# Segmented attention beside a 2-D Fourier filter: head stacks read in rows of 8 KB, and an output projection in 14 products

## The chip, the core and the metric

The kernel runs on one core of a Trainium2 chip. A core has a matrix engine (TensorE, PE in the profile, with its weight loads as PEld), a vector engine (VectorE, DVE), a scalar engine (ScalarE, ACT), GpSimd (POOL) and SyncE (SP), which does nothing here but start DMA transfers. Sixteen DMA engines move data between the device's memory (DRAM) and the on-chip memory SBUF. SBUF has 128 partitions (rows); matrix products land in PSUM, which the vector and scalar engines read. The metric is the device time of one execution in microseconds (us), lower is better.

## The reference, cut to what matters

Two independent parts stand side by side in the output. Part B multiplies a 2048 x 576 input by a filter in the space of a two-dimensional Fourier transform; the kernel computes it with matrix products against tables, and the change does not touch it. Part A is attention in four segments of 512 positions with a compressive memory, 32 heads of width 18:

```python
q,k,v = x@wq, x@wk, x@wv            # each reshaped to 32 heads x 4 segments x 512 x 18
for s in range(4):
    logits = einsum("bhqd,bhkd->bhqk", qs, ks)*scale + mask
    p = softmax(logits);  a_dot = einsum("bhqk,bhkd->bhqd", p, vs)
    pq = phi(qs)                                     # phi(t) = t+1 if t>0 else exp(t)
    a_mem = einsum(pq, M) / (einsum(pq, z) + 1e-6)   # memory of the earlier segments
    o = g*a_mem + (1-g)*a_dot
    M = M + einsum(phi(ks), vs);  z = z + sum(phi(ks))
out_A = concat(o) @ wo                               # 2048 x 576
out_B = irfft2(rfft2(xB) * (w_r + 1j*w_i))
out = concat([out_A, out_B], axis=-1)
```

The weights of the queries and keys are drawn large, so logits are large and the products must be close to float32.

## The kernel before

**Stages.** The Fourier part's forward half fills the first 73 us. Then come the projections (`projections`, line 533): for each of the four segments g, nine column tiles of 128 of the joined query and key weights (`qk_unit`, line 461), and four row tiles of the values. They end at about 282 us. Then the inverse Fourier half runs, with the first steps of the attention beside it from 294 us (the first product of line 637), and from 355 us (the first of line 682) to the end attention is all that runs (`attention`, line 913).

**Split numbers.** To get the precision of float32 out of bf16 products, each query and key value is cut in three bf16 parts, high, middle and low, which `qk_unit` writes to a tile `sp3` of 128 rows x 3 x 512 and stores in DRAM as `qkD` (line 486). The product of a query and a key is made of six of the nine part products. So that one matrix product does them all, the six pieces of 18 rows each are stacked on 108 partitions: the query stack `Qs` has parts (h,h,h,m,m,l), the key stack `Ks` parts (h,m,l,h,m,h) (`stack_dmas`, line 612). A stack holds 8 heads of a segment; there are 16 query stacks and 16 key stacks, n = 0 to 15. Each is filled by six transfers of 18 partitions, with eight pieces of 1 KB per partition (one per head). Three query and four key buffers rotate. In the trace the first buffers of both carry the name `x`.

**Attention's loop.** A step t of `attention` treats one head of one segment: `s2` makes the logits, transposed, from `Ks` and `Qs` and takes the exponential; `pv` multiplies with the values; `s1`, ten steps ahead, makes the logits a first time for the row maxima. The maxima of four heads go through GpSimd, a transpose on TensorE and a copy (`mpath`, line 655) into a tile `mts`, from which a small transfer on ScalarE's own DMA queue (line 672, 8 KB) puts them on partitions 108 and 109 of the query stack, where `s2` needs them about three steps later. Every eight steps a new n begins; its stack loads are appended to a list `q` (lines 936 to 938: queries for n+2, keys for n+3, then the values), and each step takes up to two off the list. They are issued on SP's queue, in program order, beside the stores of results (`uD`, `rD`), the loads for the memory path (`pq`, `ux`, `rr`, `rd`) and the output stores.

**Memory path and output.** `mixed` (line 794) combines the segment before (`combine`) and computes the memory term of this one (`mem1`) over five row tiles t of heads, 126 rows for t < 4 and 72 for t = 4. `combine` leaves the result split in two parts that TensorE takes at float32r, `oh` (high) and `ol` (rest). `oproj` (line 837) multiplies with the output weights, split likewise into `woh` and `wol` (`late_setup`, line 595): three products (oh woh, oh wol, ol woh) for each of the five tiles, 15 into one PSUM tile of 128 x 288, eight such units per segment, for segments 0 to 2. Half a unit is issued per background turn (`run_bg`). The last segment has its own code (`last_tile`, `last_proj`).

The order of all instructions is that in which the code issues them (`manual_schedule`), for each engine apart; engines meet at semaphores.

## Time and profile before

| what | us |
|---|---|
| median of 3 runs (717.62 to 721.08) | 720.45 |
| the profiled execution | 718.92 |
| its span, first to last instruction | 717.2 |
| TensorE busy (share of the span) | 684.1 (95%) |
| VectorE busy | 552.3 (77%) |
| ScalarE busy | 450.1 (63%) |
| GpSimd busy | 211.1 (29%) |

The span is 1.7 us shorter than the profiled execution, and that execution is 1.5 us below the median. A row of a view of groups or of the timeline names the line, the engine, the operation, and the tiles as out<-in; "x5" counts instructions put together. A bracket at its end is the time that the engine stood idle before it, and what ended that. A list of waits gives who waited for whom: total us, times, longest. Matrix products are pipelined: the next starts before the one before has ended, so the spacing of starts, not the duration, is the cost of one.

### The profile page before, as it was taken

To read this page: it belongs to the slowest core of one execution; us is meant where nothing else is said; L and a number is where in the kernel's file an instruction comes from. 1 tells how busy PE (TensorE), PEld (TensorE's weight loads), DVE (VectorE), ACT (ScalarE), POOL (GpSimd) and SP (SyncE) were. 2 spreads that over 40 slices of the span, in tenths; PEclk is the share of its full clock that TensorE was granted. 3 is DMA by queue.
4 is the path that set the end of the run, shared out by engine and by line. 5 is a ranking of instruction groups with operands and counts; after the bars stand their busy time and mean duration, and the time that the engine had idled before them with its cause. 6 is when DMAs were issued, how large, how long until landed. Compare 5 with 4: busy or idle time off the path is not lost. (4 is left out here: it accounts for less than half of the span.)

```text
span 717.2 us, 14460 instructions
## 1 busy us (share of the span) xinstructions
PE 684.1 (95%) x5007; PEld 505.7 (71%) x5007; DVE 552.3 (77%) x1270; ACT 450.1 (63%) x985; POOL 211.1 (29%) x403
## 2 busy tenths in 40 slices
PE   4999999999999999999999899899999999999997
PEld 4988869879779879999854444444466445664497
DVE  5999979899699789788588787878466876568633
ACT  3665796585586575444487677767466776567521
POOL 5432000100200111665154333435123662235300
PEclk9999999999999999999999999999999999999999
DMA  8995435645363568899547665776446775441152
GB/s 305 293 280 164 148 118 185 192 169 182 110 220 147 178 198 281 208 231 228 165 111 174 171 172 136 185 173 170 114 126 158 195 169 126 126 137 42 28 153 83
DMA packets 83304, 121.02 MB, mean 169 GB/s; under 512 B 11472, under 2 KB 50750, under 8 KB 83096
## 3 DMA queue, kind: packets, MB, share of 16 engines
q1 hardware_dynamic: 76580, 104.11, 50.3%
q0 software_dynamic: 5632, 15.76, 8.0%
q8 instruction: 39, 0.64, 0.4%
q10 hardware_dynamic: 1020, 0.25, 0.2%
q14 instruction: 33, 0.27, 0.1%
HBM read 81.78 MB, written 38.24 MB: 167 GB/s over the span
## 5 line engine op out<-in xcount | busy, mean ns | idle before, releaser
L641 DVE CUSTOM_DVE_ANT_0 junk<-s,x 128x512 bf16<-128x512 f32 (+1 forms) x256 | 141.4, 552 | 67.2 <-PE s L637 62.0
L696 POOL TENSOR_SCALAR_AFFINE_SELECT P<-P 128x512 f32<-128x512 f32 (+2 forms) x132 | 78.8, 623 | 67.3 <-ACT P L683 51.8
L647 DVE TENSOR_REDUCE mx<-s 128x4 f32<-128x512 f32 x128 | 87.7, 686 | 2.9 <-PE s L646 0.7
L683 ACT ACTIVATE P<-s 128x512 f32<-128x512 f32 x128 | 76.4, 597 | 16.5 <-PE s L682 5.4
L711 PE MATMUL pv<-P,vs 128*32 128x512 f32 (+3 forms) x1024 | 82.8, 441 | 0.0
L692 ACT ACTIVATE P<-s 128x256 f32<-128x256 f32 x128 | 49.4, 386 | 49.7 <-PE s L691 49.6
L688 ACT ACTIVATE P<-s 128x512 f32<-128x512 f32 x128 | 76.1, 594 | 2.0 <-PE s L687 1.8
L637 PE MATMUL s<-Ks,Qs 108*128 108x384 bf16 (+3 forms) x256 | 69.1, 301 | 1.2 <-DVE mx L647 0.9
L711 PEld LDWEIGHTS pv<-P,vs 128*32 128x32 f32 x1024 | 27.2, 109 | 45.3 <-issue 42.5
L459 PE MATMUL pj<-x,wqkh 128*128 128x512 f32 x162 | 56.5, 409 | 0.0
L205 DVE TENSOR_TENSOR Z<-t,t 128x290 f32<-128x290 f32 (+1 forms) x96 | 48.4, 554 | 0.1
L637 PEld LDWEIGHTS <-Qs 108*128 108x128 bf16 x320 | 31.5, 98 | 22.6 <-issue 11.3
L506 POOL MEMSET vt<- 128x32 f32 x16 | 2.4, 166 | 149.1 <-PE pm L516 127.7
L205 DVE TENSOR_TENSOR t<-Z 128x580 f32<-128x580 f32 x64 | 46.0, 755 | 0.0
L142 PE MATMUL f<-ftab,eh 128*128 128x290 f32 (+1 forms) x160 | 32.5, 322 | 12.1 <-DMA ftab<-ftab 9.5
L646 PE MATMUL s<-tri,idb 128*128 128x128 bf16 x256 | 43.2, 220 | 0.0
L295 PE MATMUL i<-civ,Y 128*128 128x256 f32 (+1 forms) x288 | 39.0, 288 | 0.2 <-POOL Y L280 0.2
L295 PEld LDWEIGHTS i<-civ,Y 128*128 128x128 f32 (+1 forms) x288 | 36.4, 181 | 1.0 <-POOL Y L280 0.4
L306 PE MATMUL i<-itab,T 128*128 128x290 f32 (+1 forms) x224 | 36.3, 305 | 0.1
L637 PE MATMUL s<-Ks,x 108*128 108x384 bf16 (+3 forms) x128 | 35.3, 306 | 1.1 <-DVE mx L647 0.6
L142 PEld LDWEIGHTS f<-ftab,eh 128*128 128x128 f32 (+1 forms) x160 | 26.2, 207 | 14.1 <-issue 8.5
L459 PE MATMUL pj<-x,wqkl 128*128 128x512 f32 x90 | 35.5, 395 | 0.0
(203 smaller groups left out, 1820.8 us busy)
## 6 DMA issues: line engine op xcount, KB each, us to landing
qkD<-sp SPq DMA_DIRECT2D x36, 384.0 KB
Ks<-qkD SPq DMA_DIRECT2D x72, 144.0 KB
x<-qkD SPq DMA_DIRECT2D x60, 144.0 KB
Qs<-qkD SPq DMA_DIRECT2D x60, 144.0 KB
xin<-xb SPq DMA_DIRECT2D x16, 384.0 KB
cfw<-cfw POOLq DMA_DIRECT2D x16, 384.0 KB, 4.4
civ<-civ POOLq DMA_DIRECT2D x16, 384.0 KB, 7.6
vs<-vD SPq DMA_DIRECT2D x16, 330.0 KB
```

Of the source, the lines that this page charges most:

```text
L142: nc.tensor.matmul(p[:,r,:FP],x,t,start=n==0,stop=n==6)
L205: v.tensor_tensor(o,a,b,op=op)
L295: nc.tensor.matmul(p[:m,k],Y[i][:,q,c*128:c*128+m],cc[:,hl,o:o+256],start=n==0,stop=n==5)
L459: s.nc.tensor.matmul(out,a,b,start=i==0,stop=i==len(L)-1)
L637: nc.tensor.matmul(out,Q[:108,h,128*i:128*i+128],K[:108,h,:128*(i+1)],start=True,stop=True)
L641: nc.vector.tensor_tensor_reduce(out=junk[:,:w],in0=src,in1=s.mask[:,512-w:],scale=1.0,scalar=-3.0e38, op0=OP.add,op1=OP.max,accum_out=s.m ...
L647: nc.vector.tensor_reduce(out=s.mx[k][:,hh],in_=pa.rearrange("p (b c) -> p b c",c=128),axis=mybir.AxisListType.X,op=OP.max)
L683: nc.scalar.activation(P[0][:,hh],p0,AF.Exp,scale=SC)
L688: nc.scalar.activation(P[1][:,hh],p1,AF.Exp,scale=SC)
L692: nc.scalar.activation(P[2][:,hh],p2,AF.Exp,scale=SC)
L696: nc.gpsimd.affine_select(out=x[:,r],in_=x[:,r],pattern=[[0,r.stop-r.start],[1,128]],compare_op=OP.is_ge,fill=0.0,base=0,channel_multiplie ...
L711: nc.tensor.matmul(s.pvt[32*hh:32*hh+32,128*j:],vt[:,j,19*h:19*h+32],mv[0][:,hh,mv[1]],start=j==0,stop=j>1,skip_group_check=True)
```

## The change

**Query and key columns are permuted on the host** so that a tile of 128 columns holds sixteen of the 18 dimensions of 8 heads, ordered dimension by head; the two dimensions left over of all 32 heads, of the queries and of the keys, make up tile 4. In DRAM, `qkD` is laid out by group of heads and by part, and the left-over rows go to a second array `reD`, once for each place that they have in a stack (six stores instead of one for tile 4). **A stack** is then filled by four transfers: 48, 32 and 16 partitions from `qkD` and 12 from `reD`, each partition one piece of 8 KB that holds all eight heads. The parts of a key are stored in reversed order, so that the same six part products arise. Stack 0 is loaded in four turns of the hook instead of six. The store of phi(q), the transposed phi(k) and their layout follow the permutation (`pqD`, `pk`).

**The output projection** has its tile 4 rearranged: the 56 rows that were empty beneath the 72 rows of `oh` take the first 56 rows of `ol`, and a second tile holds a copy of `oh`'s 72 rows and the last 16 of `ol`; the weights are doubled to match. So three products of tile 4 become two, and a unit has 14. Rows move across partitions by three transfers from SBUF to SBUF per segment. `combine`, `mem1` and the loads for them treat the tiles in the order 4, 0, 1, 2, 3 (`ORD`).

```diff
@@ -339,6 +339,7 @@
 BF=mybir.dt.bfloat16
+ORD=(4,0,1,2,3)
 H=32; DH=18; SC=float(DH)**-0.5
@@ -356,9 +357,9 @@
 def host_wo(w):
-    o=np.zeros((126,5,D),np.float32)
-    o[:,:4]=w[:504].reshape(4,126,D).transpose(1,0,2)
-    o[:72,4]=w[504:]
+    o=np.zeros((128,6,D),np.float32)
+    o[:126,:4]=w[:504].reshape(4,126,D).transpose(1,0,2)
+    o[:72,4]=w[504:]; o[72:,4]=w[504:560]; o[72:88,5]=w[560:]
     return o
@@ -389,7 +390,8 @@
         d=lambda n,sh,dt: dp.tile(sh,dt,name=n)
-        s.qkD=[d(f"qkD{i}",[1152,3,512],BF) for i in range(4)]
+        s.qkD=[d(f"qkD{i}",[8,3,128,512],BF) for i in range(4)]
+        s.reD=[d(f"reD{i}",[24,32,512],BF) for i in range(4)]
         s.pqD=[None]+[d(f"pqD{i}",[576,512],F32) for i in range(1,4)]
@@ -468,31 +470,42 @@
         if (g==0 and mt<4) or (g==3 and mt>4): r1=r0
-        nc.scalar.copy(sp3[:,0],ps)
+        j=[2,1,0] if mt>4 else [0,1,2]
+        nc.scalar.copy(sp3[:,j[0]],ps)
         if r1>r0:
...
         if r1>r0: nc.vector.scalar_tensor_tensor(e[r0:r1],ps[r0:r1],0.0,e[r0:r1],op0=OP.max,op1=OP.add)
-        nc.vector.tensor_tensor(ps,ps,sp3[:,0],op=OP.subtract)
+        nc.vector.tensor_tensor(ps,ps,sp3[:,j[0]],op=OP.subtract)
         qr=min(r1,128 if mt<4 else (64 if mt==4 else 0))
-        if qr>r0: nc.sync.dma_start(s.pqD[g][128*mt:128*mt+qr],e[:qr])
-        yield
-        nc.scalar.copy(sp3[:,1],ps)
-        yield
-        nc.tensor.matmul(ps,s.nid,sp3[:,1],start=False,stop=True,skip_group_check=True)
-        nc.scalar.copy(sp3[:,2],ps)
-        nc.sync.dma_start(s.qkD[g][128*mt:128*mt+128],sp3)
+        if qr>r0:
+            a=s.pqD[g][0]
+            J=[(18*8*mt*512,[[512,16],[18*512,8]],e[:qr])] if mt<4 else [((16+j)*512,[[18*512,32]],e[32*j:32*j+32]) for j in range(2)]
+            for o,ap,x in J: nc.sync.dma_start(bass.AP(tensor=a.tensor,offset=a.offset+o,ap=ap+[[1,512]]),x)
+        yield
+        nc.scalar.copy(sp3[:,j[1]],ps)
+        yield
+        nc.tensor.matmul(ps,s.nid,sp3[:,j[1]],start=False,stop=True,skip_group_check=True)
+        nc.scalar.copy(sp3[:,j[2]],ps)
+        if mt!=4: nc.sync.dma_start(s.qkD[g][mt-(mt>4)].rearrange("i p c -> p i c"),sp3)
+        else:
+            for r,i,c,n in ((0,0,1,3),(0,1,1,2),(0,2,1,1),(64,0,3,3),(64,0,2,2),(64,0,1,1)):
+                m={3:0,2:3,1:5}[n]; a=s.reD[g][r*12//64+2*m]
+                x=sp3[r:r+64,i:i+c] if c==n else sp3[r:r+64,i:i+1].to_broadcast([64,n,512])
+                nc.sync.dma_start(bass.AP(tensor=a.tensor,offset=a.offset,ap=[[512,64],[64*512,n],[1,512]]),x)
         if r1<=r0: return
...
         if k0>=r1: return
-        n=r1-k0; c0=128*mt+k0-576
+        n=r1-k0
         pt=pp.tile([128,4,128],F32,name="ptr",tag="pt")
...
         yield
-        nc.scalar.copy(s.pk[:,:,c0:c0+n],pt[:,:,:n])
+        pk=s.pk.rearrange("p a (h d) -> p a h d",d=18)
+        if mt==4: nc.scalar.copy(pk[:,:,:,16:],pt[:,:,:n].rearrange("p a (d h) -> p a h d",d=2))
+        else: nc.scalar.copy(pk[:,:,8*mt-40:8*mt-32,:16],pt.rearrange("p a (d h) -> p a h d",h=8))
     def v_unit(s,g,tb,tp,pp):
@@ -596,31 +609,34 @@
         s.sel=cp.tile([96,5,126],BF,name="sel",bufs=1); nc.gpsimd.dma_start(s.sel,io["sel"].rearrange("p (t m) -> p t m",t=5))
-        s.woh=cp.tile([126,5,576],F32R,name="woh",bufs=1); s.wol=cp.tile([126,5,576],F32R,name="wol",bufs=1)
-        for t in range(6):
-            if t>1: yield
-            if t<5:
-                x=cp.tile([128,576],F32,name="ob")[:126]; q.append(x)
+        s.woh=cp.tile([128,5,576],F32R,name="woh",bufs=1); s.wol=cp.tile([128,5,576],F32R,name="wol",bufs=1)
+        for t in (0,1,2,3,5,4,6):
+            if t: yield
+            if t<6:
+                x=cp.tile([128,576],F32,name="ob"); q.append((t,x))
                 nc.sync.dma_start(x,io["wo"][:,576*t:576*t+576])
-            for _ in range(2): yield
-            if t>0:
-                x=q.pop(0)
-                nc.scalar.copy(s.woh[:,t-1],x)
-                nc.gpsimd.tensor_tensor(s.wol[:,t-1],x,s.woh[:,t-1].bitcast(F32),op=OP.subtract)
+            yield
+            if t!=5: yield
+            if len(q)>(t<6):
+                u,x=q.pop(0)
+                if u==5: nc.scalar.copy(s.wol[64:96,4],x[64:96]); continue
+                r=128 if u<4 else 72
+                nc.scalar.copy(s.woh[:,u],x)
+                nc.gpsimd.tensor_tensor(s.wol[:r,u],x[:r],s.woh[:r,u].bitcast(F32),op=OP.subtract)
         yield
...
         L=[]
-        T,base,order=((s.Qs[n%3],0,(0,0,0,1,1,2)),(s.Ks[n%4],576,(0,1,2,0,1,0)))[qk]
-        for pc,o in enumerate(order):
-            a=s.qkD[g][base+8*G*18:base+8*G*18+18,o]
-            ap=bass.AP(tensor=a.tensor,offset=a.offset,ap=[[1536,18],[1536*18,8],[1,512]])
-            def go(T=T,pc=pc,ap=ap):
-                nc.sync.dma_start(T[18*pc:18*pc+18],ap)
-                if pc==5: s.loaded.add((n,qk))
-            L.append(go)
+        T=(s.Qs[n%3],s.Ks[n%4])[qk]
+        u=G+4*qk
+        for p0,i0,i1 in ((0,0,3),(48,qk,2+qk),(80,2*qk,1+2*qk)):
+            L.append(lambda p0=p0,i0=i0,i1=i1: nc.sync.dma_start(T[p0:p0+16*(i1-i0)].rearrange("p a c -> p (a c)"),s.qkD[g][u,i0:i1].rearrange("i (d h) c -> (i d) (h c)",h=8)))
+        def go():
+            nc.sync.dma_start(T[96:108],s.reD[g][12*qk:12*qk+12,8*G:8*G+8])
+            s.loaded.add((n,qk))
+        L.append(go)
         return L
@@ -798,7 +814,7 @@
             if i>=d:
-                for _ in s.mem1(g,i-d): yield
+                for _ in s.mem1(g,ORD[i-d]): yield
     def ux_load(s,g,t):
@@ -812,16 +828,21 @@
             r=126 if u<4 else 72
-            s.oh[u]=tp.tile([126,512],F32R,name="oh",bufs=5); s.ol[u]=tp.tile([126,512],F32R,name="ol",bufs=5)
+            s.oh[u]=tp.tile([128,512],F32R,name="oh",bufs=5); s.ol[u]=tp.tile([128,512],F32R,name="ol",bufs=5)
             (nc.vector.tensor_copy if s.now>=119 else nc.scalar.copy)(s.oh[u][:r],s.am[u][:r])
...
             r=126 if u<4 else 72
-            eng().tensor_tensor(s.ol[u][:r],s.am[u][:r],s.oh[u][:r].bitcast(F32),op=OP.subtract)
+            A,B=s.oh[u],s.ol[u]
+            l=B if u<4 else tp.tile([128,512],F32R,name="ol4",bufs=1)
+            eng().tensor_tensor(l[:r],s.am[u][:r],A[:r].bitcast(F32),op=OP.subtract)
+            if u==4:
+                s.later(1,lambda: nc.sync.dma_start(B[:72].bitcast(F32),A[:72].bitcast(F32)))
+                s.later(2,lambda: (nc.sync.dma_start(A[72:128].bitcast(F32),l[:56].bitcast(F32)),nc.sync.dma_start(B[72:88].bitcast(F32),l[56:72].bitcast(F32))))
         late=g==2
         for t in range(7+late):
-            if t>1 and not late: high(t-2); low(t-2)
+            if t>1 and not late: high(ORD[t-2]); low(ORD[t-2])
             if t<5:
-                r=126 if t<4 else 72; x=xs[t]
+                i=t; t=ORD[t]; r=126 if t<4 else 72; x=xs[t]
                 pb=s.post("pb")
@@ -830,9 +851,10 @@
                     eng().tensor_tensor(s.am[t][:r],x[:r],s.am[t][:r],op=OP.add)
-                if t<2: s.later(1,lambda t=t: s.ux_load(g,t+3))
-            if late and 1<t<7: high(t-2)
-            if late and t>2: low(t-3)
+                t=i
+                if t<2: s.later(1,lambda t=t: s.ux_load(g,ORD[t+3]))
+            if late and 1<t<7: high(ORD[t-2])
+            if late and t>2: low(ORD[t-3])
             yield
@@ -843,11 +865,10 @@
                 w=slice(288*hf,288*hf+288)
-                L=[(a,b,t) for a,b in ((oh,s.woh),(oh,s.wol),(ol,s.woh)) for t in range(5)]
-                for i,(a,b,t) in enumerate(L):
-                    r=126 if t<4 else 72
-                    nc.tensor.matmul(ps,a[t][:r,c],b[:r,t,w],start=i==0,stop=i==14)
-                    if i==7: yield
+                L=[(a,b,t,126) for a,b in ((oh,s.woh),(oh,s.wol),(ol,s.woh)) for t in range(4)]+[(oh,s.woh,4,128),(ol,s.wol,4,88)]
+                for i,(a,b,t,r) in enumerate(L):
+                    nc.tensor.matmul(ps,a[t][:r,c],b[:r,t,w],start=i==0,stop=i==13)
+                    if i==6: yield
                 nc.scalar.copy(ob[:,w],ps)
@@ -909,7 +930,7 @@
 
-        for n,t,b in (("oh",F32R,5),("ol",F32R,5),("am",F32,5),("pq",F32,5),("ux",F32,3)): s.tp.tile([128 if b==3 else 126,512],t,name=n,bufs=b)
+        for n,t,b in (("oh",F32R,5),("ol",F32R,5),("am",F32,5),("pq",F32,5),("ux",F32,3),("ol4",F32R,1)): s.tp.tile([128 if n in ("oh","ol","ux","ol4") else 126,512],t,name=n,bufs=b)
     def attention(s,tp,ps):
@@ -937,14 +958,14 @@
             st=t%32
-            if 16<=t<21: s.pq_load(1,t-16)
+            if 16<=t<21: s.pq_load(1,ORD[t-16])
             if t==34: bg.append(s.den(1,lane))
...
                         next(r); yield
-                    for u in range(3): s.ux_load(g-1,u)
+                    for u in range(3): s.ux_load(g-1,ORD[u])
                     yield from r
@@ -1045,8 +1066,11 @@
     f=lambda a: np.asarray(a,np.float32)
-    return dict(xa=host_xa(f(x)),wqk=host_wt(np.concatenate([f(wq),f(wk)],1)).reshape(128,-1),wv=host_wt(f(wv)).reshape(128,-1),
-        wo=host_wo(f(wo)).reshape(126,-1),beta=np.repeat(f(beta),4).reshape(128,1),**atables())
+    h,d=np.arange(32),np.arange(16)
+    m=[((8*G+h[None,:8])*18+d[:,None]).ravel() for G in range(4)]; r=(h*18+16+d[:2,None]).ravel()
+    wqk=np.concatenate([f(wq)[:,np.concatenate(m+[r])],f(wk)[:,np.concatenate([r]+m)]],1)
+    return dict(xa=host_xa(f(x)),wqk=host_wt(wqk).reshape(128,-1),wv=host_wt(f(wv)).reshape(128,-1),
+        wo=host_wo(f(wo)).reshape(128,-1),beta=np.repeat(f(beta),4).reshape(128,1),**atables())
 def emit(nc,tc,io):
@@ -1080,7 +1104,7 @@
                     if g==3 and i==3: A.masks()
-                    if g==3 and 0<i<7:
+                    if g==3 and 0<i<5:
                         for _ in range(2): q0.pop(0)()
```

In these excerpts of the order, a row is a line, an operation, the tiles as out<-in and the shape; equal neighbours are counted ("x6").

SP's queue at the start of the block n = 3 (its loads fill a query buffer and a key buffer, here `Qs_3293` and `Ks_3295`, after the change `Qs_3316` and `Ks_3318`), before:

```order
L621 DMA Qs_3293<-qkD_71 18x8x512 x6
L621 DMA Ks_3295<-qkD_71 18x8x512 x3
L722 DMA rD_3305<-U 4x2x512
L621 DMA Ks_3295<-qkD_71 18x8x512
L727 DMA uD_3301<-U 18x2x512
L621 DMA Ks_3295<-qkD_71 18x8x512
L727 DMA uD_3301<-U 18x2x512
L621 DMA Ks_3295<-qkD_71 18x8x512
L727 DMA uD_3301<-U 18x2x512
L628 DMA vs<-vD_78 128x4x165
L727 DMA uD_3301<-U 18x2x512
```

The same place on SP's queue after:

```order
L635 DMA Qs_3316<-qkD_71 48x4096
L635 DMA Qs_3316<-qkD_71 32x4096
L635 DMA Qs_3316<-qkD_71 16x4096
L637 DMA Qs_3316<-reD_75 12x4096
L635 DMA Ks_3318<-qkD_71 48x4096
L635 DMA Ks_3318<-qkD_71 32x4096
L635 DMA Ks_3318<-qkD_71 16x4096
L637 DMA Ks_3318<-reD_75 12x4096
L644 DMA vs<-vD_82 128x4x165
L738 DMA rD_3328<-U 4x2x512
L743 DMA uD_3324<-U 18x2x512 x4
```

Both stacks now stand ahead of the store of the sums (`rD`), which waits for the result copy `U`; before, three of the twelve loads stood behind it.

TensorE's queue in the output projection of segment 2, two units, before:

```order
L849 MATMUL po<-woh,oh 128x288 x5
L849 MATMUL po<-wol,oh 128x288 x5
L849 MATMUL po<-woh,ol 128x288 x5
L849 MATMUL po<-woh,oh 128x288 x5
L849 MATMUL po<-wol,oh 128x288 x5
L849 MATMUL po<-woh,ol 128x288 x5
```

The same two units after:

```order
L870 MATMUL po<-woh,oh 128x288 x4
L870 MATMUL po<-wol,oh 128x288 x4
L870 MATMUL po<-woh,ol 128x288 x4
L870 MATMUL po<-woh,oh 128x288
L870 MATMUL po<-wol,ol 128x288
L870 MATMUL po<-woh,oh 128x288 x4
L870 MATMUL po<-wol,oh 128x288 x4
L870 MATMUL po<-woh,ol 128x288 x4
L870 MATMUL po<-woh,oh 128x288
L870 MATMUL po<-wol,ol 128x288
```

Tile 4 has moved from the fifth place of each group of five to two products at the end of the unit.

The three moves of rows for segment 0 on SP's queue, after (before, these rows are not there, and the loads of `pq` and the stack follow the stores of `uD` directly):

```order
L743 DMA uD_3325<-U 18x2x512 x2
L839 DMA ol<-oh 72x512
L743 DMA uD_3325<-U 18x2x512
L840 DMA oh<-ol_6394 56x512
L840 DMA ol<-ol_6394 16x512
L772 DMA pq<-pqD_79 72x512
L635 DMA x_2754<-qkD_72 48x4096
```

The moves stand ahead of a `pq` load and of the next block's stack loads.

## The prediction

> **What bounds the kernel now.** I read the page's engine row, then busy time by stage, then TensorE's waits in the attention.
>
> ```profile
> PE 684.1 (95%) x5007; PEld 505.7 (71%) x5007; DVE 552.3 (77%) x1270; ACT 450.1 (63%) x985; POOL 211.1 (29%) x403
> 20.00:360.00 340.00, 334.54 (x2137) 295.86 (x2137) 292.81 (x562) 213.26 (x427) 69.67 (x144) 1.00 0.64 194
> 365.00:505.00 140.00, 132.11 (x1159) 65.89 (x1157) 113.19 (x340) 104.85 (x253) 58.26 (x108) 1.00 0.65 162
> 510.00:556.00 46.00, 46.00 (x396) 31.27 (x394) 26.95 (x79) 27.53 (x67) 13.32 (x28) 0.98 0.50 131
> 597.00:645.00 48.00, 47.96 (x406) 32.05 (x408) 29.25 (x85) 29.86 (x72) 13.77 (x30) 1.00 0.47 128
> 677.00:717.00 40.00, 35.47 (x261) 33.44 (x261) 14.62 (x23) 8.75 (x21) 2.92 (x6) 0.99 0.34 109
> ```
>
> The last five rows are stages: length, busy time of PE, PEld, DVE, ACT, POOL, then the granted clock, the mean busy share of the 16 DMA engines and GB/s. TensorE is the bound, busy 95% of the span at full clock. It never stops in the two stretches that hold the output projections of segments 0 and 1 (46.00 of 46.00, 47.96 of 48.00). In 365 to 505 us it stands idle for 7.9 us. What it waits for from 365 to 690 us:
>
> ```profile
> PE s L682 <- DMA Qs<-mts: 3.2, 3, 1.4
> PE pd L765 <- DMA pq<-pqD: 1.4, 1, 1.4
> PE pb L826 <- DMA rr<-rrD: 1.2, 1, 1.2
> PE s L637 <- DMA Qs<-qkD: 0.4, 1, 0.4
> PE s L682 <- DMA x<-mts: 0.2, 1, 0.2
> ```
>
> These five rows, 6.4 us, are all waits for transfers. So two things can move the time: fewer products where TensorE is full, and transfers that land sooner or later than the step that needs them.
>
> **One product less per unit.** Three segments have eight units each, so 24 products go. Their price is the spacing of starts:
>
> ```profile
> 681.04 0.83 PE L849 MATMUL po<-woh,oh 126*128 126x288 f32 x5
> 681.70 0.82 PE L849 MATMUL po<-wol,oh 126*128 126x288 f32 x5
> 682.37 0.83 PE L849 MATMUL po<-woh,ol 126*128 126x288 f32 x5
> 683.03 0.30 PE L849 MATMUL po<-woh,oh 126*128 126x288 f32 x1
> ...
> 689.34 0.69 DVE L859 TENSOR_TENSOR ux<-ux,pb 126x512 f32<-126x512 f32 x1 [8.48 <-DMA ux<-uD]
> 691.82 0.40 PE L849 MATMUL po<-woh,oh 126*128 126x288 f32 x1 [0.16 <-ACT ob L851]
> ```
>
> Fifteen products take 683.03 - 681.04 = 1.99 us, 0.133 each. In the two full stretches 16 products are worth 2.1 us. Segment 2's eight units lie in the tail. There VectorE waits until 689.34 for `ux`, ScalarE's copies that free the accumulators stand behind the work that follows, and TensorE meets that at 691.82. So the six units ahead of 691.82 end sooner for nothing: the wait grows by their 0.8 us. The two units behind it give 0.27. The term is -2.4; its ends are -2.1 (tail nothing) and -3.2 (all 24).
>
> **The three moves of rows, and the new tile order.** The first low part is made on GpSimd at 471.7 us and the first product that could read it starts at 512.2:
>
> ```profile
> L819 POOL TENSOR_TENSOR ol<-am,oh x10: 1260/1268/1282, 471.7 to 593.1; 126x512 fp32r<-126x512 f32 x8, 72x512 fp32r<-72x512 f32 x2
> L849 PE MATMUL po<-woh,oh x120: 290/295/489, 512.2 to 694.7; 126*128 126x288 f32 x96, 72*128 72x288 f32 x24
> ```
>
> With tile 4 first, the moves have about 40 us; the cover is gone only if they took longer. In SP's queue they wait for that GpSimd operation, 1.27 us, ahead of a `pq` load and the next stack loads; issued a step or two after it, they find it done. I take 0, at worst 1 us per segment.
>
> **Projections.** Tile 4 is stored by six transfers instead of one, and three `pqD` stores split: 20 + 3 more issues on SP at 0.33 us, 7.6 us in all over 200 us in which SP mostly waits; who waits for these rows reads them many us later. The copies of `pk` read PSUM with a stride now:
>
> ```profile
> L486 SPq DMA_DIRECT2D qkD<-sp x36: 319/326/384, 82.8 to 273.4; - x36
> L495 ACT COPY pk<-ptr x15: 357/588/622, 100.5 to 225.5; 128x512 f32<-128x512 f32 x12, 128x256 f32<-128x256 f32 x3
> PE pj L484 <- ACT sp L482: 1.9, 3, 1.0
> ```
>
> No row has a strided copy out of PSUM. From below it costs what it does now; if it took double, ScalarE would be busy 12 x 0.588 + 3 x 0.357 = 8.1 us more, beside a TensorE that has lost 1.9 us to ScalarE in this stage. I take 0 (as many elements as before) and keep +2 for the range.
>
> **The stack loads.** What six loads of 18 partitions cost, in a stretch with almost nothing else (534.7 to 540.5 us), against a stretch of transfers of 128 partitions (22 to 38 us); below them SP's issues of one block:
>
> ```profile
> DMA packets 775, 0.75 MB, mean 130 GB/s; under 512 B 54, under 2 KB 774, under 8 KB 774
> q1 hardware_dynamic: 774, 0.74, 57.1%
> DMA packets 1858, 4.71 MB, mean 294 GB/s; under 512 B 202, under 2 KB 202, under 8 KB 1857
> 407.93 4.65 SPq L621 DMA_DIRECT2D Qs<-qkD  x6
> 412.62 1.88 SPq L621 DMA_DIRECT2D Ks<-qkD  x3
> ```
>
> 57.1% of 16 engines is 9.1: a load of 18 partitions keeps nine engines busy and moves 130 GB/s, so a stack of 885 KB drains in 6.8 us. For rows of 8 KB from SP's queue there is no row. The bounds are 130 GB/s (nothing won) and 294 GB/s (3.0 us a stack). The partitions are still few per transfer, so I lean to the lower: 180 GB/s, about 5 us a stack. [...]
>
> Who gains by it? The maxima (`mts`) are the ones that come late:
>
> ```profile
> 372.67 0.65 ACTq L672 DMA_DIRECT2D Qs<-mts  x1
> 371.15 1.84 SPq L621 DMA_DIRECT2D x<-qkD  x5
> DMA packets 787, 0.82 MB, mean 153 GB/s; under 512 B 50, under 2 KB 740, under 8 KB 786
> q10 hardware_dynamic: 34, 0.01, 4.3%
> 380.26 0.39 PE L682 MATMUL s<-Qs,Ks 110*128 110x512 bf16 x1 [0.97 <-DMA Qs<-mts]
> 390.10 0.62 ACTq L672 DMA_DIRECT2D Qs<-mts  x1
> 397.88 0.39 PE L682 MATMUL s<-Qs,Ks 110*128 110x512 bf16 x1 [1.40 <-DMA Qs<-mts]
> ```
>
> `mts` is issued at 372.67, 1.5 us after five stack loads. The third and fourth rows are the DMA views of 372.70 to 378.05 (787 packets, none of queue q10, which is `mts`) and 378.05 to 379.55 (all 34 of q10). So the small transfer waits behind what was issued ahead of it. TensorE would have gone on at 379.29, 6.6 us after the issue; at 390.10 the same sum gives 6.4. A landing within about 6.4 us costs nothing.
>
> After the change, SP puts four transfers of the query stack there in the time of four small ones, and the key stack follows at once. Two us after the block's start at 0.34 us per issue, five or six are out: 885 KB and one or two of 393 and 262 KB, some 1.3 to 1.5 MB. At 180 GB/s that drains in 7.2 to 8.3 us, less the 2 gone: 5.2 to 6.3, just inside. In block n = 1 a weight load that waits for GpSimd now stands behind the first transfer alone, so its 0.97 goes. I count as won that 0.97, the 0.4 and 0.2 of the last two rows of waits, and half of the 1.4 for `pq`, 2.3 us; the other waits I leave.
>
> **Sum.** -2.4 - 2.3 = -4.7 against the profiled 718.92: 714.2. The median of the three runs is 1.5 above that execution, so 715.7 on its scale.
>
> **Rivals.**
>
> *The maxima come later (slower).* The same numbers decide it: with 1.4 MB ahead, the edge is a drain of 6.4 + 2 = 8.4 us, 167 GB/s. At 150 GB/s the drain takes 9.3 us, and `mts` is late by 0.9 us in each of 13 blocks: +11.7, less the 3.4 of today's two rows of `mts`, so +8.3; with the product term -2.4, 718.92 + 5.9 + 1.5 = 726.3. At 140 it is 1.6 us each, +17.4, 735. For it: about 130 is what the stack loads show, SP ran at most nine loads in 6.6 us before and can now put out two stacks in 3 us, and the query and key stacks both stand ahead of other work. Against it: many blocks have a `pq`, `ux` or `ry` load between, which waits and spaces the stacks; and of the two `mts` per block, the second meets an emptier queue. [...]
>
> *The loads are hidden anyway (same).* Drain rate and landing change, but stalls move only from one block to another, as the 6.4 us are single events of 0.2 to 1.4. Then the products alone count: 718.92 - 2.4 + 1.5 = 718.0.
>
> **How the numbers follow.** A measurement of this kernel, whose runs span 0.5%, tells about 3.6 us from nothing. The forecast, 715.7 (on its own 711 to 716.9, from all 24 products and all transfer waits gone, -9.6, to just beyond the mark), has 0.46. The hidden case at 718 has 0.22. The late maxima have 0.32: the edge lies so near to my drain rate that either side is open, and it counts once for each block. For 8 in 10 the range goes down to 711 and up to 729, past 726.3 and towards the 735 that 140 GB/s would give. So faster 0.46, same 0.22, slower 0.32.
>
> **What would show it.** Each step right: 24 fewer products of line 849 at 0.133 us spacing, and the two full stretches about 1 us shorter each; a stretch of stack loads alone at 16 engines and 160 GB/s or more; waits for `Qs<-mts` at or below 3.4 us. Wrong: `Qs<-mts` at 0.5 us or more in most blocks; `pk` copies well over 0.59 us with a longer wait of TensorE for ScalarE before 230 us; a wait of `po` for `oh` or `ol`.

## The result, and the profile after

The changed kernel is slower: 724.22 us (median of 22 runs, 718.56 to 728.61) against 719.89 (22 runs, 714.56 to 728.79), a ratio of 1.0063 with a 95% interval of 1.0043 to 1.0083. Ratios, here and below, use only the runs within 1.5% of the fastest of their kernel, medians use all, so a ratio can differ from the quotient of its two medians. The forecast was 715.7, on the other side. The profiled execution took 721.03 us with a span of 719.3, 2.1 above the span of before; it lies 3.2 below its median, so a second profile of the unedited kernel was taken (725.47 us, span 723.8).

The engine row and the same five stages of the changed kernel (columns as before):

```profile
PE 683.1 (95%) x4983; PEld 502.7 (70%) x4983; DVE 551.9 (77%) x1270; ACT 450.8 (63%) x986; POOL 211.1 (29%) x403
20.00:360.00 340.00, 333.42 (x2127) 294.94 (x2126) 291.52 (x556) 212.61 (x425) 69.38 (x144) 1.00 0.71 198
365.00:505.00 140.00, 130.53 (x1134) 65.86 (x1133) 111.20 (x336) 104.09 (x251) 58.19 (x107) 0.99 0.82 165
510.00:556.00 46.00, 45.57 (x377) 30.16 (x378) 26.91 (x78) 27.86 (x68) 13.31 (x28) 1.00 0.53 117
597.00:645.00 48.00, 47.15 (x399) 30.32 (x391) 28.20 (x83) 29.59 (x72) 13.54 (x30) 1.00 0.53 123
```

24 products are gone, and TensorE is idle for longer: 9.5 us in 365 to 505 (7.9 before), and no longer without a gap in the two stretches of output projections (the work lies some 3 us later in them, and waits for `pq` at 510 and 601 fall in). The DMA engines are busier there (0.82 against 0.65) for nearly the same GB/s.

TensorE's waits from 365 to 690 us, the four largest of the first profile, and then of the second:

```profile
PE s L698 <- ACT P L699: 2.8, 4, 2.0
PE pb L847 <- DMA rr<-rrD: 2.4, 1, 2.4
PE s L698 <- DMA x<-mts: 2.2, 2, 1.6
PE pd L781 <- DMA pq<-pqD: 2.2, 2, 1.4
```

```profile
PE s L698 <- DMA x<-mts: 4.2, 2, 3.3
PE s L698 <- DMA Qs<-mts: 3.0, 4, 1.4
PE pd L781 <- DMA pq<-pqD: 2.6, 2, 1.6
PE pb L847 <- DMA rr<-rrD: 2.1, 1, 2.1
```

The three waits for transfers of the first list are 6.8 us; with the one of 2.0 at 402.89, which goes back to a transfer too (below), 8.8. The second list has 11.9. Before, the five rows of waits for transfers came to 6.4.

**Where the time went.** The start of the same product in both traces, after minus before, tells where the kernel falls behind (times of the kernel before): -0.1 us at 333, +1.0 at 338 (a wait of 0.93 for VectorE's `yout`), 0.0 at 382 (the first wait for `mts` is gone), +2.3 at 417, +2.4 at 460, +4.8 at 470 (`rr`), +3.4 at 492, +2.3 at 555 (the first full stretch gained 1.0), +4.1 at 606 (a second wait for `pq`), +3.1 at 644 (the second stretch gained 1.1), +2.1 at the end.

**How a transfer stops ScalarE.** Timelines of the changed kernel, SP's issues, then ScalarE's issue and next instruction, then TensorE:

```profile
391.99 1.98 SPq L635 DMA_DIRECT2D Ks<-qkD  x2
394.94 0.31 SPq L772 DMA_DIRECT2D pq<-pqD  x1
396.31 0.30 SPq L635 DMA_DIRECT2D Ks<-qkD  x1
396.88 0.29 SPq L637 DMA_DIRECT2D Ks<-reD  x1
397.81 0.31 SPq L772 DMA_DIRECT2D pq<-pqD  x1
398.22 0.39 SPq L644 DMA_DIRECT2D vs<-vD  x1
399.80 0.56 SPq L738 DMA_DIRECT2D rD<-U  x1
401.58 0.62 ACTq L688 DMA_DIRECT2D x<-mts  x1
402.24 0.60 ACT L699 ACTIVATE P<-s 128x512 f32<-128x512 f32 x1 [3.38 <-DMA Ks<-qkD]
402.89 0.38 PE L698 MATMUL s<-Qs,Ks 110*128 110x512 bf16 x1 [1.99 <-ACT P L699]
```

In this program the transfers of SP and ScalarE take eight semaphores in turn (542 transfers in the trace, 67 or 68 on each). So at most eight are under way, and the issue of the next waits until the one eight places back in the program has landed: the `mts` transfer of 401.58 has the first `Ks` of 391.99 eight places ahead of it, and that landed at 401.50. ScalarE stood 3.38 us at this issue, its next instruction starting behind it at 402.24; TensorE lost 1.99. I call a transfer *held* when it is issued within 0.35 us of the landing of the one eight places back. From 365 to 690 us, 153 of 354 transfers were held before, 80 of 315 in the changed kernel.

### The profile page after: what moved, and what is told of

It is laid out like the page before. It is cut to its first block, busy times and chain, and to the rows that moved or that the text cites. A ratio compares the mean times of both kernels' runs of the same rounds, so it can differ in the third digit from the quotient of the medians.

```text
span 719.3 us, 14404 instructions
## 1 busy us (share of the span) xinstructions
PE 683.1 (95%) x4983; PEld 502.7 (70%) x4983; DVE 551.9 (77%) x1270; ACT 450.8 (63%) x986; POOL 211.1 (29%) x403
## 4 chain that ended last, share of the span: by engine, by line
PE 73%; DMA 10%; DVE 8%; ACT 4%; issue 4%; POOL 1%; SPq 0%; DVEq 0%; ACTq 0%; POOLq 0%
PE pj L461 14%; PE pv L727 8%; PE s L653 8%; PE pjv L461 8%; PE po L870 5%; PE i L295 4%; PE i L306 4%; DMA pq<-pqD 3%; PE s L698 3%; PE s L702 2%; PE f L142 2%; PE pn L800 2%; PE po L899 2%; PE pm L529 2%; PE s L662 1%
```

## The experiments

All ratios are to the kernel before, run beside each on the same chip, with 95% intervals. "Idle" is TensorE's from 365 to 690 us, 13.1 before and 15.5 after. The expectations name their theories by letters: A (the loss is the stack loads') against P (the projection's), then B (the burst in which the loads are issued) against R (their rows of 8 KB), then S (the limit of eight). The edits shown are cut to the lines that matter.

| run | median, before beside it | ratio | idle | held |
|---|---|---|---|---|
| e1 products alone | 726.30, 721.78 | 1.0080 [1.0045, 1.0114] | 20.1 | 155/359 |
| e2 stacks alone | 726.61, 721.78 | 1.0060 [1.0024, 1.0097] | 17.5 | 73/294 |
| e3 changed, paced | 719.91, 721.78 | 0.9957 [0.9920, 0.9994] | 13.8 | 32/315 |
| e4 changed, quiet | 719.37, 721.78 | 0.9942 [0.9911, 0.9973] | 12.5 | 30/315 |
| e6 e1, mts by SP | 725.95, 719.72 | 1.0090 [1.0054, 1.0125] | 16.1 | 146/358 |
| e7 e3, pq spread | 716.08, 719.72 | 0.9967 [0.9932, 1.0002] | 12.2 | 25/315 |
| e8 e3, 15 products | 720.40, 719.72 | 1.0016 [0.9975, 1.0057] | 13.2 | 27/300 |
| e9 e1, pq spread | 723.61, 721.12 | 1.0022 [0.9989, 1.0055] | 18.1 | 145/362 |
| e10 before, pq spread | 721.75, 721.12 | 0.9988 [0.9953, 1.0022] | 12.2 | 118/354 |
| e11 e7, early, path a step sooner | 726.53, 721.12 | 1.0074 [1.0043, 1.0105] | 14.3 | 39/314 |
| e12 e4 with e11's edits | 725.15, 721.12 | 1.0047 [1.0013, 1.0080] | 17.9 | 41/306 |
| e13 e7, early | 712.45, 719.35 | 0.9923 [0.9889, 0.9958] | 10.5 | 22/319 |
| e14 e7, seven transfers a stack | 725.06, 719.35 | 1.0031 [0.9989, 1.0073] | 14.6 | 131/384 |
| e15 before, three moves | 722.11, 719.35 | 1.0028 [0.9995, 1.0061] | 14.6 | 168/364 |
| e16 before, tile order | 723.30, 719.35 | 1.0043 [1.0005, 1.0082] | 13.4 | 133/354 |
| e17 e13, 15 products | 714.97, 721.04 | 0.9907 [0.9875, 0.9939] | 12.2 | 21/304 |
| e18 e13, rr ahead of ux | 709.75, 721.04 | 0.9845 [0.9801, 0.9889] | 7.3 | 35/321 |

### Each half of the change alone (e1, e2, e5)

e1 is the kernel before with the projection's part of the diff (`ORD`, `host_wo`, `late_setup`, `combine`, `oproj`); e2 is the changed kernel with the old text of these; e5 is the changed kernel unedited.

> The kernel before with the output projection in 14 products alone (tile order 4, 0, 1, 2, 3 and the three moves of rows with it); stacks and their layout as before. Theory A (the loss comes from the stack loads): the two full stretches are about 1 us shorter each as in the changed kernel, so 719.9 - 2.2 = 717.7 us, a ratio to before of 0.997 (0.9955 to 0.9985), and no wait of a product po for oh or ol. Theory P (the new order of tiles and the moves take back what the products give): 720 us or more, ratio 1.000 to 1.004, with new waits in lines of the memory path (pb, pd, po).

> The changed kernel with the output projection of before (15 products, tiles in the order 0 to 4, no moves of rows); stacks of 8 KB rows stay. Theory A: all of the loss and none of the gain, 724.2 + 2.2 = 726.4 us, ratio to before 1.009 (1.006 to 1.012). Theory P: most of the loss goes with the projection, 720 to 722 us, ratio 1.000 to 1.003.

> The changed kernel once more, unedited, for a second profile: the first one (span 719.3) lies 3 us below the median span of its runs. If the waits are fixed by the order of issue, the same ones appear (402.9 us ScalarE held 2.0, x<-mts 2.2, rr 2.4) and the additional time is in the same places; if they are chance, others take their place. Expected: the same places, 1 to 4 us more in total.

Both halves lose alone, and together they lose no more than one of them: neither A nor P describes it. In e1, TensorE's waits from 365 to 690 us, and then two of ScalarE's from 365 to 505 (the engine and line that waited, for whom; us in total, times, longest):

```profile
PE s L686 <- ACT P L687: 7.0, 8, 1.9
PE s L686 <- DMA Qs<-mts: 2.6, 1, 2.6
PE s L686 <- DMA x<-mts: 2.0, 2, 1.3
```

```profile
ACT P L687 <- DMA x<-qkD: 4.9, 2, 2.5
ACT P L687 <- DMA vs<-vD: 3.7, 1, 3.7
```

With six small loads a stack, the additional transfers of the projection reach a queue that is already held at 153 of 354; ScalarE is stopped at its own issues, 8.6 us by these two rows (0.7 for `x<-qkD` before), and TensorE loses 7.0 (1.3 before). The share of held transfers is as before (155 of 359), so the count alone does not tell. In e2 only 73 of 294 are held, and the maxima are late instead, as the first rival had it; e2's waits of TensorE:

```profile
PE s L694 <- DMA Qs<-mts: 6.9, 5, 2.5
PE s L694 <- DMA x<-mts: 2.3, 2, 1.5
```

e5 has the waits of the first profile at the same places (`x<-mts` near 419, `rr` near 472, two of `pq`), and others near 400: the stop of 1.99 us at 402.89 is not among them, TensorE waits there for ScalarE for 0.82. So that stop is one event of one execution. The span is 4.5 us longer, a little over the upper end of its expectation.

### Spreading the stack loads (e3, e4)

```diff
-            if q: q.pop(0)()                  # second slot of a step
+            if q and hh==2: q.pop(0)()        # e3
+            if q and hh>1: q.pop(0)()         # e4; its first slot: if q and hh!=1
```

> The changed kernel with stack loads taken off the list at one per step and a second one only in the steps with hh = 2: a block's nine loads go out over eight steps of 2.7 us in place of four and a half. Theory B (burst: what is issued behind 0.9 to 1.5 MB of stacks waits for their drain at 150 GB/s): the waits x<-mts (2.2 us), the stop of ScalarE at the issue of a maxima transfer (2.0), the additional 1.2 of rr and 0.8 of pq mostly go, 718 to 720 us, ratio to before 0.997 to 1.000. Theory R (rows of 8 KB hold all 16 engines, and others land later in whatever order they are issued): 723 to 725 us, ratio 1.004 to 1.008, the same waits at other places.

> The changed kernel with no stack load issued in the second half of step hh = 0 and in step hh = 1, at whose end the maxima transfers are issued; both slots of steps hh = 2 and 3 are used, so a block's loads still go out in two bursts of five. Theory B, in its form that only what lies directly ahead of the maxima counts: 717.5 to 720 us, ratio 0.996 to 1.000, waits for mts below 0.5 us together, rr and pq as in the changed kernel (2.4 and 2.2). Theory R: 723 to 726 us, ratio 1.004 to 1.009. If it is the later query stack that decides, a wait of s1 (line 653) for qkD or reD appears, and the time is above 724.

Same rows, same bytes, other moments: the loss turns into a small gain (e3's interval ends at 0.9994), 32 and 30 transfers are held, and theory R falls. So the loss of the changed kernel comes from the moments at which its stack loads are issued. What is left in each is one large wait near 403 us and `rr`; the first two rows are e3's, the other two e4's:

```profile
PE s L698 <- DMA Qs<-mts: 6.1, 2, 4.9
PE pb L847 <- DMA rr<-rrD: 1.4, 1, 1.4
```

```profile
PE s L653 <- DMA Qs<-reD: 3.3, 1, 3.3
PE pb L847 <- DMA rr<-rrD: 2.4, 1, 2.4
```

Keeping away from the maxima bought nothing over even spacing; the 3.3 us is the late query stack that e4's last sentence named, without the time above 724 that it put to it.

### Who is held, and by how many (e6, e14)

```diff
-        else: s.later(2,lambda: nc.scalar.dma_start(out,mt))    # e6, on e1
+        else: s.later(2,lambda: nc.sync.dma_start(out,mt))
-        for p0,i0,i1 in ((0,0,3),(48,qk,2+qk),(80,2*qk,1+2*qk)):    # e14, on e7
+        for p0,i0,i1 in ((0,0,1),(16,1,2),(32,2,3),(48,qk,1+qk),(64,1+qk,2+qk),(80,2*qk,1+2*qk)):
```

> The kernel with the 14 products alone, its maxima transfers issued by SP's queue at the same place of the program in place of ScalarE's. Theory S (SP's and ScalarE's transfers share eight semaphores in turn, so that ScalarE, which works in order, stands still until the transfer eight places back has landed; the additional transfers of the change shift these places): the 7.0 us of s waiting for ScalarE's P go, the waits for mts stay at 3 to 5 us, 719 to 722 us, ratio to before 0.996 to 1.001. Rival T (the maxima are late because of the data ahead of them, and it does not matter who issues): waits for mts grow by what ScalarE's waits lose, 725 to 728 us, ratio 1.005 to 1.010.

> The paced kernel with spread pq loads, its stacks filled by seven transfers of 16 and 12 partitions in place of four (same rows of 8 KB, same bytes, two transfers per step). Theory S (eight transfers at most are under way on SP's and ScalarE's queues together; the issue of a ninth waits for the landing of the first): the share of transfers from 365 to 690 us that are issued at the moment at which the one eight places back lands goes from 25 of 315 to above 100 of some 400, and the time to 720 us or more, ratio to before above 0.999. Theory D (only the bytes ahead count): 715 to 717 us, ratio 0.992 to 0.997.

TensorE's waits in e6:

```profile
PE pd L769 <- DMA pq<-pqD: 3.3, 2, 1.8
PE s L641 <- DMA Ks<-qkD: 2.8, 1, 2.8
PE s L686 <- DMA Qs<-mts: 2.5, 2, 1.6
PE s L686 <- ACT P L687: 0.8, 3, 0.4
```

The waits for ScalarE go from 7.0 to 0.8, so S names their cause; up to 510 us the same product starts 5.0 us earlier than in e1. But SP is now held with the transfers behind it, `pq` and `Ks` come late, and the time is T's number (its mechanism is not: the waits for `mts` fell). e14 has e7's rows and bytes in more transfers: a block's fifteen loads go out two in each step, and so, like e7's nine, over its eight steps. Held rises from 25 to 131, the ratio from 0.9967 to 1.0031, while the DMA engines are as busy from 365 to 690 us as in e7 (0.64 and 0.63), so the smaller transfers do not take more of the engines' time. TensorE's largest waits in this stretch are for what stands behind the stacks:

```profile
PE pd L781 <- DMA pq<-pqD: 3.8, 2, 3.3
PE pb L847 <- DMA rr<-rrD: 2.4, 1, 2.4
```

That is what theory S expected of count, ratio and time; the two intervals overlap a little, the medians are 5.7 and -3.6 us from the kernel before beside them. One part of the loss is not shown to come from the limit: e14 also loads stack 0, and the stacks ahead of the attention, in other turns, and of the 8.5 us between the two spans 3.2 are lost near 290 us, at a wait of 2.03 for ScalarE and a stretch at half clock behind it.

### The crowded place at 365 to 405 us (e7, e9, e10)

```diff
-            if 16<=t<21: s.pq_load(1,ORD[t-16])
+            if t in (18,21,24,27,30): s.pq_load(1,ORD[t//3-6])
```

> The paced kernel with the five first pq loads at t = 18, 21, 24, 27, 30 in place of 16 to 20, where they stand among a block's stacks and the loads of wo. If the largest wait left (4.9 us at 402.6, Qs<-mts, whose transfer took 11.7 us) comes from these 1.2 MB: it goes to below 1 us, 715 to 717 us, ratio to before 0.989 to 0.994. If it comes from the stacks and the wo loads alone, it stays at 3 us or more, 718.5 to 720.5, ratio 0.995 to 0.998; and if den, at t = 34, now has to wait for pq, a wait of pd appears there.

> The kernel with the 14 products alone and the five first pq loads at t = 18, 21, 24, 27, 30. Theory C (crowding at 365 to 405 us: the additional load of wo, 295 KB, falls among 1.2 MB of pq and the block's stacks, transfers there take 8 to 10 us, and ScalarE and TensorE are held; a hold of 1.4 us or more also lets the granted clock fall to half for 3.4 us): the waits of 1.7 at 393 and 2.6 at 400 go, 717 to 720.5 us, ratio to before 0.996 to 1.000. Theory M (the moves and the new tile order at 455 to 500 and 570 to 600 us are what costs): the time stays at 723 or more, ratio above 1.004.

> The kernel before with the same shift of its pq loads, as a control: it loses its wait of 1.4 us at 397.9 and the 1.0 at 380.3 at most, 717.5 to 719.5 us, ratio to before 0.996 to 1.000. If the crowding at 365 to 405 costs the kernel before as much as the changed one, 714 to 716 and the change has no part in it.

On e3 the edit takes the wait of 4.9 us away (largest left: 1.6); against the kernel before beside each, the medians say 1.8 us, and by the ratios the gain is not settled. The kernel before does not gain by it. e9 lies between its two theories: it keeps 7.7 us of waiting for ScalarE, which C had going, but its ratio is 1.0022 where e1 had 1.0080, and the two intervals overlap. How much of e1's loss the crowding is stays open.

### What the products cost, and bring (e8, e15, e16, e17)

e15 adds three transfers per segment from `oh` and `ol` of tile 4 into tiles nobody reads; e16 has `ORD` in `mem1`, `combine` and their loads; e8 and e17 are e3 and e13 with the projection of before.

> The kernel before, 15 products and tiles in the order 0 to 4, with three transfers per segment added from oh and ol of tile 4 into tiles that nothing reads (72 x 512, 56 x 512 and 16 x 160 numbers), at the places of the program that the moves of rows have. Theory M (the moves cost, in the queue that is full anyway, what the products bring): 723 to 726 us, ratio 1.003 to 1.008. Else 719 to 721, ratio 0.997 to 1.002.

> The kernel before with the order of tiles 4, 0, 1, 2, 3 in the memory path alone (15 products, no moves of rows, no sixth load of wo). If the order of the loads of pq and ux is what costs: 723 to 726 us, ratio 1.003 to 1.008. Else 719 to 721, ratio 0.997 to 1.002; with the moves at 1.000 as well, the sixth load of wo between 365 and 400 us is what is left of the products' price.

> The paced kernel with the output projection of before (15 products, tiles 0 to 4). It gives what the 14 products are worth once the loads are paced: by the two full stretches and the tail 2.2 to 2.4 us, so 722.2 us, ratio to before 0.999 (0.996 to 1.002). If other waits absorb the products, 720 us as the paced kernel; if the change of the projection costs waits here as it does alone, this is faster than the paced kernel, 715 to 718.

> The fastest kernel so far (paced stack loads, pq loads spread, stack loads of the inverse stage even over 30 turns; 712.45 us) with the output projection of before (15 products, tiles 0 to 4, no moves, no sixth load). If the 14 products are worth the 2.8 us that the milestones of TensorE show once the waits are few: 715.3 us, ratio to before 0.996 (0.993 to 1.000). If the moves and the order of tiles still cost what they cost alone (1.003 and 1.004): 712 us or less, ratio 0.989 to 0.992.

The new order of tiles costs by itself, with no product more or less, though its interval begins at 1.0005; the moves may (their interval includes 1). Where they cost is not shown: both were profiled in executions below their medians (719.04 and 720.60 us). Together they come to 0.7%. e1's 0.8% is what is left after its products' gain: the two full stretches are 2.1 us shorter in it too, and with the tail that is some 0.4%. So about 0.5% remain for the sixth load of `wo`, which was not tried alone, and for what the parts do to each other, each figure being uncertain by 0.3 to 0.4%. What the 14 products are worth in the end stays open: +0.6% by e3 and e8, nothing by e13 and e17, each within the intervals.

### Two more edits, and the fastest kernel (e11, e12, e13, e18)

```diff
-                for _ in range(1+(i%24==0)):          # prologue: e11, e12, e13, e18
-                    if q: q.pop(0)()
+                if 7*(i+1)//10>7*i//10: q.pop(0)()
-                    for i in range(8):                # recip's chain, e11 and e12
-                        next(r); yield
+                    for i in range(9):
+                        next(r)
+                        if i<8: yield
+                    next(r)                           # e18: same step, rr ahead of ux
                     for u in range(3): s.ux_load(g-1,ORD[u])
+                    yield
                     yield from r
```

> The changed kernel with paced stack loads in the attention, pq loads spread, in the inverse stage 21 stack loads evenly over 30 turns (they were in the first 20), and rr loaded ahead of the three ux (0.77 MB) that stood in front of it. Each goes at one wait of TensorE that was left: yout at 339 (0.7 to 1.5 us) and rr at 468 (1.6). If waits are worth what they show, 716 - 2 = 713 to 714.5 us, ratio to before 0.990 to 0.994; if they only move on, 715.5 to 717 as before these two edits.

> The same three edits on the kernel whose stack loads keep away from the maxima (no load in the second half of step hh = 0 and in hh = 1). If only what lies directly ahead of the maxima counts, its waits for mts are below 0.5 us and it is at 712 to 714 us, under the paced one; if even spacing counts, 714 to 717 us, with a wait for a late query stack near 403.

> The paced kernel with spread pq loads and, of the edits of the two kernels that lost, only the first: 21 stack loads evenly over the 30 turns of the inverse stage; rr again behind the three ux. If the loss came from moving rr (the memory path then starts a step earlier, among other loads), this is at 714 to 716 us, ratio to before 0.989 to 0.996, without the 0.7 to 1.5 us wait for yout at 339. If it came from the later stacks of the inverse stage, 720 us or more.

> The same fastest kernel with the load of rr put ahead of the three ux loads in the same step, everything else in its order (the two slower variants had also begun the memory path a step earlier). If what stood in front of rr is its price: the wait of 1.5 us at 464.4 goes, 710.5 to 712 us, ratio 0.987 to 0.993. If moving rr was itself the harm, and not the step: 718 us or more.

e11 lost 9 us against e7, each taken against the kernel before beside it; e13 takes its first edit alone and is 6.9 us under the kernel before by the medians; e18 puts `rr` first without starting the memory path a step sooner, and gains. So the step did the harm. The traces of e11 and e13, which differ in it alone, show where: the same products of the attention start 1.5 us earlier in e11 at 480 us, 2.4 later at 510 (behind a wait of 1.94 for `mts` at 486.59), 1.7 later at 550 and 8.5 later at 590, so most is lost where the memory path of the next segment runs. It is lost with few transfers held, 39 of 314: a low count alone does not make a kernel fast. e12 lost as well; its waits for `mts`, expected below 0.5 us together, are 9.2, one of them 5.3. Waits of e11, and the largest two of e18:

```profile
PE s L698 <- DMA Qs<-mts: 5.0, 5, 1.9
PE pb L847 <- DMA rr<-rrD: 1.4, 1, 1.4
```

```profile
PE s L698 <- DMA x<-mts: 1.1, 1, 1.1
PE s L698 <- ACT P L699: 0.8, 3, 0.4
```

e18, 709.75 us, is 1.55% under the kernel before (0.9845, 0.9801 to 0.9889), with both halves of the change in it. `rr` is gone from its waits.

## Why the prediction was wrong

**The product term was right.** First and last product of a stretch, in groups by tile, before and then after (min/median/max ns, first to last start in us):

```profile
L849 PE MATMUL po<-woh,oh x40: 290/296/489, 512.2 to 550.6; 126*128 126x288 f32 x32, 72*128 72x288 f32 x8
L849 PE MATMUL po<-woh,ol x40: 290/294/301, 515.0 to 553.3; 126*128 126x288 f32 x32, 72*128 72x288 f32 x8
```

```profile
L870 PE MATMUL po<-woh,oh x40: 290/295/483, 515.5 to 555.5; 126*128 126x288 f32 x32, 128*128 128x288 f32 x8
L870 PE MATMUL po<-wol,ol x8: 292/292/294, 518.7 to 555.7; 88*128 88x288 f32 x8
```

From first to last the stretch goes from 41.11 to 40.12 us, the second from 40.00 to 38.89: 2.10 us, where 2.1 was forecast. After 674 us another 1.0 is gained, 0.27 forecast.

**The copies of `pk` were right:** 12 of them take 597 ns now (588 before), and TensorE's wait for ScalarE there is 1.9 us in both traces.

```profile
L508 ACT COPY pk<-ptr x12: 567/597/631, 103.7 to 225.4; 128x512 f32<-128x512 f32 x12
L507 ACT COPY pk<-ptr x3: 383/400/402, 100.3 to 206.4; 128x256 f32<-128x256 f32 x3
```

**The drain was near.** The 108 rows of one stack pass between 537.37 and 542.95 us, where the DMA view of the changed kernel says:

```profile
DMA packets 349, 1.01 MB, mean 180 GB/s; under 512 B 74, under 2 KB 240, under 8 KB 241
q1 hardware_dynamic: 348, 0.99, 101.3%
```

All 16 engines are occupied (101.3%) in place of nine (57.1%). The stack's own 885 KB in 5.58 us are 159 GB/s; the forecast was 180. By my own edge of 167 the maxima should have been late.

**They were late, but not in 13 blocks.** The first rival charged 0.9 us to each; its 726.3 came nearer to the measured 724.22 than the forecast, by a wait that mostly did not occur. The changed kernel has two such waits in its first profile (2.2 us) and six in the second (7.2). The second rival, hidden anyway, is not what happened: the waits are neither those of before nor as many.

**The step that failed** is the second term of the sum: "I count as won ... 2.3 us; the other waits I leave." It leaves 4.1 us of waits; the profile has 8.8, and 0.9 for `yout`. These 5.6 us, less the 0.7 that the products brought beyond the forecast, are 4.9 of the 6.8 between the forecast profile of 714.2 and the 721.03 measured; the other 1.9 are not put down to a wait here. The 0.97 and the 0.4 were indeed won. `pq` grew from 1.4 to 2.2 where half was to go, `rr` from 1.2 to 2.4, and ScalarE's stop of 2.0 was new. I had treated the waits as a list from which single ones may be struck. The runs show one queue of eight in their place: which step finds its transfer late depends on when the transfers ahead of it were issued (e3: held from 80 to 32, ratio from 1.0063 to 0.9957) and on how many they are (e14: held from 25 to 131, ratio from 0.9967 to 1.0031), so waits moved from place to place. Spacing alone was worth 1.06% between e3's ratio and that of the changed kernel, each to its own runs of the kernel before. The mark of 3.6 us between a gain and nothing rested on three runs that span 0.5%; the 22 runs of the kernel before span 2.0%.

**The new order of tiles at 0** failed too, and the moves at 0 perhaps: I looked at the products that read these rows, 40 us later, and not at the queue the transfers pass through. The order alone is 1.0043, some 3 us; the bound of 1 us per segment was for the moves alone. That the queue is where it costs is likely from e3 and e14, but not shown for these edits.

## What to carry to other kernels

Count transfers as well as bytes: with eight under way at most, 153 of 354 issues here came within 0.35 us of the landing of the one eight places back (80 of 315 after the change), and ScalarE, which issues the maxima itself, stood 3.38 us at one of them. A block's loads belong spread over the block; here spacing the stack loads took the same work from +0.6% to -0.4%, and with the other transfers spaced and reordered (e18) to -1.6%. A change that only removes products can lose (e1, 1.0080), and reordering loads alone can cost (e16, 1.0043), so what is added to a queue or moved in it is to be priced there and not only at its reader.

## What had not been expected

**Behind some of TensorE's waits its granted clock was 0.50 for 3.41 us.** The stretches ahead of, in and behind 3.4 us of the changed kernel (granted clock third from the end), after TensorE's wait of 2.38 us for `rr` up to 470.00:

```profile
466.30:469.70 3.40, 1.32 (x18) 0.53 (x17) 1.24 (x5) 0.74 (x2) 1.81 (x3) 1.00 1.11 207
469.70:473.10 3.40, 3.10 (x13) 1.67 (x13) 2.17 (x5) 1.60 (x4) 0.63 (x1) 0.50 0.94 170
473.10:476.50 3.40, 3.40 (x34) 1.75 (x33) 2.80 (x9) 2.60 (x6) 0.41 (x1) 1.00 0.93 147
```

The clock is 0.50 for 3.41 us; 13 products run in it, 34 in the 3.4 us behind (not all of one size). In the 20 profiles there are 24 such stretches from 20 to 700 us (3.41 us, or twice that); every one lies at a wait of TensorE of 1.35 us or more. Of 26 waits of 1.8 us or longer, 20 have one, of 31 between 1.3 and 1.8 five, of 125 between 0.7 and 1.3 one; so the edge of 1.4 us that e9's expectation names is not one: the kernel before has a stretch behind a wait of 1.42 up to 507.13, the changed kernel none behind 1.99 up to 402.89. The length of a wait does not sort them by itself. The stretches of one trace lie on a grid of 3.413 us: in e14 they begin at 289.15, 470.05 and 511.01, 53.0 and 12.0 such steps apart. In the step of the grid right ahead of a stretch, TensorE was idle for 53% or more in 23 of the 24 cases (61% in the first row above; 42% in the other case, 508.11 in the kernel before), and no step as idle lacks a stretch behind it; the most idle one without, in e5 at 418.0, has 52%. These are counts; what sets the clock down, and why some stretches last two steps, no run shows. The wait of 1.60 at 417.18 in the changed kernel has none behind it: in its step, 415.09 to 418.50, TensorE is busy for 1.81 of 3.41 us.

A long wait can so cost up to 1.7 us beyond itself (an estimate, half of the 3.41 us at 0.50): over the 22 runs of the changed kernel time and granted clock correlate at -0.70 (718.56 us at 0.998, 728.61 at 0.993), and e13 and e18, whose longest waits after 290 us are 1.5 and 1.1 us, have no such stretch. No run sets the length of a wait on purpose, so the dependence is observed, not tested.
